# The first token block's attention, pair by pair of heads: a fused attention, dense and routed feed-forward kernel on one core

## The chip, the cores and the metric

One core of a Trainium2 chip runs the kernel. Its engines work side by side, each through its own instructions in order: TensorE (PE; PEld is its weight load), VectorE (DVE), ScalarE (ACT), GpSimd (POOL), and SyncE (SP), which here only issues DMAs. The metric is the device time of one execution in microseconds (us); the median of three timed executions of the kernel before is 759.19 us (756.44 to 760.04).

## The reference, cut to what matters

```python
def _attn_ref(q, k, v, g_norm):                     # q, k, v: 4 batches, 8 heads, 576 tokens, 64 wide
    kv = np.einsum('bhsd,bhse->bhde', k, v)
    out = np.einsum('bhsd,bhde->bhse', q, kv)
    rms = np.sqrt(np.mean(out * out, axis=-1, keepdims=True) + 1e-06)
    return (out / rms * g_norm).astype(np.float32)
...
def _moe_ref(x, w_in, w_out):                       # x: 2304 tokens x 512, w_in: 512 x 2048
    h = x @ w_in
    r = np.maximum(h, 0.0)
    return ((r * r) @ w_out).astype(np.float32)
...
    x = np.ascontiguousarray(attn_out.transpose(0, 2, 1, 3)).reshape(B * S, H * D)
    x = _moe_ref(x=x, **moe_kwargs)
    return _moe2_ref(x=x, **moe2_kwargs)            # eight experts, one per token, capacity 576
```

## The kernel before

The 2304 tokens are cut into six blocks of 384 (three tiles of 128). The first phase has, for each block, linear attention and then the dense feed-forward network with its 16 chunks `f` of the hidden layer; the second phase is the routed layer. Only the first block's start is touched by the change.

**Attention.** Two heads make a pair, so there are four pairs (`NPAIR`). `load_kv(0, p)` loads a pair's k and v (320 KB each), `load_q(t)` a tile's q for all pairs (256 KB). `kv(0, p)` makes a pair's 128 by 128 product in five matmuls and copies its two diagonal blocks to `kvb`, one by ScalarE (L212), one by VectorE (L213). Then, tile by tile and for all four pairs at once: `attn_out(t)` multiplies q with `kvb` (L228), ScalarE squares the result (L236), VectorE sums the squares per head (L238), GpSimd makes the mean and its power of -1/2 (L240, L242); `attn_mul(t)` scales (L246, VectorE); `attn_tr(t)` transposes on TensorE (L255) and leaves the block `xT` in two parts, a rounded one by ScalarE (L259) and the remainder by VectorE (L260).

**Weights.** The dense layer's weights come as 64-bit floats. `cvt_m(f)` turns the two tiles of chunk `f` (w_in and w_out, 128x512 each) to 32 bits: ScalarE scales the high words (L168, one each), VectorE has three kinds of integer operation (L169 and L170 on both tiles at once, 1024 columns; L174 for each). `split_m(f)` makes a rounded part (ScalarE, L183) and the remainder (GpSimd, L184). `mm1(s)` is a unit of the first product: twelve matmuls (L274), which need `xT` and both parts of w_in; its activation goes ScalarE, VectorE, ScalarE, VectorE (L282, L284, L285, L286); `mm2(s)` (L293) follows two units later. Units run (0, 0) to (0, 3), and from there chunks of blocks 0 and 1 alternate.

**What sets the order.** In this part only SyncE's queue stands as written; the other engines' orders are chosen by a scheduler when the program is built, and each engine then runs its own list in order. SyncE has at most eight loads under way.

Of the kernel before, what the change touches and what calls it, by code (L numbers as in the profile page):

```python
# [26 lines left out]
def attn_moe_kernel(ctx: ExitStack, tc: tile.TileContext, cap, kp, vp, qt, gn, wm, wg, wgt, w1, w2, ident, tri, out):  # L27
# [84 lines left out]
    def after_scatters(dma):  # L112
        dma = getattr(dma, "ins", dma)
        for i in scattered["disp"]:
            tc.add_manual_dep(
                dma, i.name, mybir.DependencyInfo(mybir.DependencyClass.Sync, mybir.DependencyReason.DATA),
                reason="reads what the scatters wrote",
            )

# [31 lines left out]
    def cvt_m(f):  # L151


        ws = [stg.pop(("m", f, i)).bitcast(I32).rearrange("p (n t) -> p n t", t=2) for i in range(2)]
        if f < 12:
            h = wpool2.tile([P, 2, 512], F32, tag="w", name="ch")
            o = wpool2.tile([P, 2, 512], F32, tag="w", name="cf")
            parts = [(h, o, slice(0, 2))]
            cvt[f] = [o[:, i, :] for i in range(2)]
        else:  # L160
            hs = [(apool1, apool)[i].tile([P, 1, 512], F32, tag="qx"[i], name="ch") for i in range(2)]
            os = [(apool, apool1)[i].tile([P, 1, 512], F32, tag="kv"[i], name="cf") for i in range(2)]
            parts = [(hs[i], os[i], slice(i, i + 1)) for i in range(2)]
            cvt[f] = [o[:, 0, :] for o in os]
        for h, o, sl in parts:
            hi, oi = h.bitcast(I32), o.bitcast(I32)
            for n, w in enumerate(ws[sl]):
                nc.scalar.activation(out=h[:, n, :], in_=w[:, :, 1].bitcast(F32), func=AF.Copy, scale=2.0 ** -112)  # L168
            nc.vector.tensor_scalar(oi, hi, -(1 << 31), None, op0=ALU.bitwise_and)  # L169
            nc.vector.scalar_tensor_tensor(  # L170
                out=oi, in0=hi, scalar=3, in1=oi, op0=ALU.logical_shift_left, op1=ALU.bitwise_or
            )
            for n, w in enumerate(ws[sl]):
                nc.vector.scalar_tensor_tensor(  # L174
                    out=oi[:, n, :], in0=w[:, :, 0], scalar=29, in1=oi[:, n, :],
                    op0=ALU.logical_shift_right, op1=ALU.bitwise_or,
                )

    def split_m(f, pool):
        os = cvt.pop(f)  # L180
        for o, d in zip(os, (wi, wo)):
            w = d[f] = pool.tile([P, 2, 512], F32R, tag="w", name="w")
            nc.scalar.copy(w[:, 0, :], o)  # L183
# [22 lines left out]
    def kv(b, p):  # L206
        k, v = kt.pop((b, p)), vt.pop((b, p))
        ps = misc()
        for c in range(NCH):
            nc.tensor.matmul(ps[:, :P], lhsT=k[:, c, :], rhs=v[:, c, :], start=c == 0, stop=c == NCH - 1)  # L210
# [54 lines left out]

    gt = {}

    def mm1(s):
# [3 lines left out]
        for c in range(KD):  # L272
            for a, m in PASSES:
                nc.tensor.matmul(  # L274
# [3 lines left out]
                n += 1  # L278

# [250 lines left out]
    with tc.manual_schedule(engines={mybir.EngineType.SP}):  # L530
# [16 lines left out]
        for p in range(NPAIR):  # L547
            load_kv(0, p)
            if p == 0:
                nc.sync.dma_start(out=id_sb, in_=ident)  # L550
                nc.sync.dma_start(out=gn_sb, in_=gn)
        for t in range(TB):
            load_q(t)
        load_m(0)
# [10 lines left out]
        for p in range(NPAIR):  # L565
            kv(0, p)
        for t in range(TB):
            attn_out(t)
        for t in range(TB):
            attn_mul(t)  # L570
            attn_tr(t)
        for f in range(2):
            cvt_m(f)
            split_m(f, wpool)
# [102 lines left out]
        for s in range(len(units)):  # L677
# [6 lines left out]
            if j == 0 and f + 2 < NF:  # L684
                cvt_m(f + 2)
# [8 lines left out]
            for p_ in plan.pop(s, []):  # L694
                p_()
            fl = s - at[NB - 1, 0]
# [379 lines left out]
```

## Time and profile before

| | |
|---|---|
| timed executions, median | 759.19 us (756.44 to 760.04) |
| profiled execution | 755.1 us |
| its span, first to last instruction | 753.2 us |
| mean granted TensorE clock in it | 0.991 of full |
| PE, DVE, ACT, POOL busy, share of the span | 95%, 49%, 41%, 39% |

The profiled execution is 1.9 us longer than its span and is the fastest of the four. The shares are means over stages with different limits: over the span TensorE is nearly always busy, but the first 72 us are another matter, and all of the change lies in these.

### The profile page before, as it was taken

The numbers are of one execution on the slowest core, as the hardware profiler recorded it, in microseconds if no ns is written. First come the engines' busy times: TensorE is split into PE (matmuls) and PEld (weight loads), VectorE is DVE, ScalarE is ACT, GpSimd is POOL, SyncE is SP. The second block draws the span as 40 slices with busy tenths as digits, with TensorE's granted clock in tenths as the row PEclk, the third lists the DMA queues.
The fourth block names the chain that finished last, engine by engine and source line by source line (L and its number), as shares of the span: only waits on it lengthen the run. The fifth ranks groups of instructions, "written<-read, shape, count | busy, mean of one in ns | idle before, by whom it ended". The sixth has DMA issues, their size and how long they took to land. (4 is left out here: it accounts for less than half of the span.)

```text
span 753.2 us, 12061 instructions
## 1 busy us (share of the span) xinstructions
PE 715.7 (95%) x4012; PEld 637.5 (85%) x4012; DVE 371.6 (49%) x833; ACT 309.5 (41%) x650; POOL 292.3 (39%) x288
## 2 busy tenths in 40 slices
PE   6678999999999999999999999999999999999985
PEld 6667999898899989989898988897888898889764
DVE  2989866548982594349634973331043221133011
ACT  2455454323222332233233264244276544376362
POOL 2566333112022200220130089043469746386881
PEclk9899999999999999999999999999999999999999
DMA  9946798401032202210010176043537554456530
GB/s 326 378 169 201 264 364 293 150 15 67 1 112 87 67 1 70 88 29 0 15 57 1 49 241 204 26 150 121 171 102 219 199 170 148 149 188 212 180 129 19
DMA packets 38016, 102.36 MB, mean 136 GB/s; under 512 B 4451, under 2 KB 4707, under 8 KB 37920
## 3 DMA queue, kind: packets, MB, share of 16 engines
q1 hardware_dynamic: 34912, 91.99, 36.4%
q0 software_dynamic: 3008, 9.10, 3.2%
q8 instruction: 59, 0.97, 0.5%
q14 instruction: 37, 0.30, 0.1%
HBM read 77.78 MB, written 23.91 MB: 135 GB/s over the span
## 5 line engine op out<-in xcount | busy, mean ns | idle before, releaser
L274 PE MATMUL pk<-xT,w 128*128 128x384 f32 x1152 | 223.1, 341 | 8.5 <-POOL w L184 4.6
L293 PE MATMUL pk<-w,g 128*128 128x512 f32 x864 | 218.4, 394 | 2.5 <-ACT g L285 2.5
L274 PEld LDWEIGHTS pk<-xT,w 128*128 128x128 f32 x1152 | 201.5, 188 | 18.6 <-POOL w L184 5.8
L195 POOL TENSOR_TENSOR w<-st,w 128x512 fp32r<-128x512 f32 x128 | 161.5, 1295 | 83.1 <-ACT w L191 83.0
L293 PEld LDWEIGHTS pk<-w,g 128*128 128x128 f32 x864 | 160.2, 188 | 31.7 <-ACT g L285 3.1
L282 ACT ACTIVATE rr<-pk 128x384 f32<-128x384 f32 x96 | 47.1, 492 | 153.6 <-PE pk L274 153.4
L817 PE MATMUL hb<-x,w 128*128 128x256 f32 (+2 forms) x672 | 96.7, 303 | 0.3
L817 PEld LDWEIGHTS hb<-x,w 128*128 128x128 f32 x672 | 93.8, 189 | 1.1 <-issue 0.2
L284 DVE TENSOR_TENSOR pk<-pk,rr 128x384 f32<-128x384 f32 x96 | 54.0, 563 | 74.6 <-ACT rr L282 73.7
L871 DVE SCALAR_TENSOR_TENSOR g<-hb,g 128x576 fp32r<-128x576 f32 (+3 forms) x72 | 40.5, 585 | 97.5 <-ACT g L870 96.5
L103 POOL DMA_INDIRECT disp<-y,sli x18 | 19.1, 1059 | 173.0 <-DVE sli L410 52.9
L355 DVE SCALAR_TENSOR_TENSOR junk<-y,wgb 128x512 f32<-128x512 f32 x120 | 78.0, 684 | 0.7 <-ACT y L313 0.6
L191 ACT CAST w<-st 128x512 fp32r<-128x512 f32 x128 | 71.7, 620 | 13.8 <-DMA st<-in_w 13.4
L285 ACT CAST g<-pk 128x384 fp32r<-128x384 f32 x96 | 46.0, 480 | 72.6 <-DVE pk L284 71.0
L286 DVE TENSOR_TENSOR g<-pk,g 128x384 fp32r<-128x384 f32 x96 | 53.3, 556 | 36.7 <-ACT g L285 36.0
L184 POOL TENSOR_TENSOR w<-cf,w 128x512 fp32r<-128x512 f32 x32 | 47.3, 1494 | 60.9 <-ACT w L183 56.3
L903 PE MATMUL hb<-w,g 128*128 128x512 f32 x264 | 65.7, 407 | 3.1 <-DVE g L871 2.5
L903 PEld LDWEIGHTS hb<-w,g 128*128 128x128 f32 x264 | 50.0, 193 | 15.7 <-DVE g L871 3.4
L870 ACT ACTIVATE g<-hb 128x576 fp32r (+3 forms) x72 | 34.9, 513 | 33.9 <-PE hb L817 29.2
L103 POOL DMA_INDIRECT out<-o,meta x22 | 21.3, 970 | 42.0 <-ACT o L911 17.8
L919 DVE SCALAR_TENSOR_TENSOR o<-bk,meta,o 64x512 f32<-64x512 f32 x3 | 2.3, 752 | 69.5 <-ACT o L918 51.0
L240 POOL TENSOR_SCALAR ms<-ss 128x8 f32<-128x8 f32 x18 | 4.6, 254 | 77.6 <-DVE ss L238 77.3
(138 smaller groups left out, 648.8 us busy)
## 6 DMA issues: line engine op xcount, KB each, us to landing
st<-in_w SPq DMA_DIRECT2D x64, 512.0 KB
st<-in_wm SPq DMA_DIRECT2D x32, 512.0 KB
disp<-zrow SPq DMA_DIRECT2D x9, 1028.0 KB
xr<-disp SPq DMA_DIRECT2D x32, 257.0 KB
k<-in_kp SPq DMA_DIRECT2D x16, 320.0 KB
v<-in_vp SPq DMA_DIRECT2D x16, 320.0 KB
q<-in_qt SPq DMA_DIRECT2D x18, 256.0 KB
out<-zrow SPq DMA_DIRECT2D x9, 512.0 KB
```

The lines of the kernel that those rows point to most:

```text
L184: nc.gpsimd.tensor_tensor(w[:, 1, :], o, f32(w[:, 0, :]), op=ALU.subtract)
L191: nc.scalar.copy(w[:, 0, :], s[:, i, :])
L195: e.tensor_tensor(w[:, 1, :], s[:, i, :], f32(w[:, 0, :]), op=ALU.subtract)
L274: nc.tensor.matmul(h, lhsT=wi[f][:, a, c * P:(c + 1) * P], rhs=xT[j][:, m, c, :], start=n == 0, stop=n == 3 * KD - 1,)
L282: nc.scalar.activation(out=r, in_=h, func=AF.Relu)
L284: nc.vector.tensor_tensor(h, h, r, op=ALU.mult)
L285: nc.scalar.copy(g[:, 0, :], h)
L286: nc.vector.tensor_tensor(g[:, 1, :], h, f32(g[:, 0, :]), op=ALU.subtract)
L293: nc.tensor.matmul(ysets[j == 1][i], lhsT=g[:, a, i * P:(i + 1) * P], rhs=wo[f][:, m, :], start=f == 0 and n == 0, stop=f == NF - 1 and n ...
L355: nc.vector.scalar_tensor_tensor(out=junk, in0=yt[j * TB + i][:, :DM], scalar=1.0, in1=wgb[e // 2][:, e % 2, :], op0=ALU.mult, op1=ALU.mul ...
L817: nc.tensor.matmul(h, lhsT=w1_at(e, f // 2, a, c)[:, f % 2 * P:(f % 2 + 1) * P], rhs=x[:, m, c, o:o + w], start=k == 0, stop=k == 3 * KD - 1,)
L903: nc.tensor.matmul(ps[:k, :], lhsT=lhs(f, a), rhs=we2[e, f][:, b, :], start=n == 0, stop=n == len(passes) * NF2 - 1,)
```

## The change

The first block's attention goes pair by pair instead of tile by tile. The three q tiles are loaded right after the first pair's k and v, ahead of the other three pairs. New functions treat one pair over all three tiles (384 tokens): `first_out` (product, square), `first_red` (sum of squares and power, on 6 columns instead of 8), `first_mul`, `first_tr` (three transposes and the rounded part of `xT`), `first_low` (the remainder). Their order is written out by hand, and the whole first section, up to the first chunk's weights, now stands as written on every engine. The first chunk's conversion is cut into its two tiles (512 columns each), w_in's put between pair 2's and pair 3's last steps. `in_order` keeps the later conversions behind the attention on ScalarE, and the second batch's `kv` products behind the first unit of `mm1` on TensorE.

```diff
+    def in_order(later, first):
...
+        tc.add_manual_dep(
+            later, first.name, mybir.DependencyInfo(mybir.DependencyClass.NoSync, mybir.DependencyReason.SCHED_ONLY),
...
-            parts = [(h, o, slice(0, 2))]
+            parts = [(h[:, a:a + n], o[:, a:a + n], slice(a, a + n)) for a, n in (((0, 1), (1, 1)) if f == 0 else ((0, 2),))]
...
+            if "kv" in marks:
+                in_order(a, marks["kv"])
...
+    def first_out(p):
+        ps = ops[p] = misc()
+        for t in range(TB):
+            nc.tensor.matmul(
+                ps[:, t * P:(t + 1) * P], lhsT=qtt[t][:, p, :], rhs=kvb[0][:, p, :],
+                start=t == 0, stop=t == TB - 1, skip_group_check=True,
+            )
...
+        nc.scalar.activation(out=x, in_=ps[:, :BT], func=AF.Square)
+
+    def first_red(p):
...
+        nc.vector.tensor_reduce(out=ss, in_=x.rearrange("p (h e) -> p h e", e=DH), axis=AX.X, op=ALU.add)
...
+        nc.gpsimd.tensor_scalar(ms, ss, 1.0 / DH, 1e-6, op0=ALU.mult, op1=ALU.add)
...
+        nc.gpsimd.tensor_tensor(r, ms, expo[:, :2 * TB], op=ALU.pow)
+
+    def first_mul(p):
...
+        nc.vector.tensor_tensor(
+            xst[p].rearrange("p (h e) -> p h e", e=DH), ps[:, :BT].rearrange("p (h e) -> p h e", e=DH),
...
+    def first_tr(p):
...
+        for t in range(TB):
+            nc.tensor.transpose(ps[:, t * P:(t + 1) * P], x[:, t * P:(t + 1) * P], id_sb)
...
+        marks["first"] = nc.scalar.activation(out=d[:, 0, p, :], in_=ps[:, :BT], func=AF.Copy, scale=gn_sb)
...
+    def first_low(p):
+        d, ps = xt_tile(0), ops.pop(p)
+        nc.vector.scalar_tensor_tensor(
+            out=d[:, 1, p, :], in0=ps[:, :BT], scalar=gn_sb, in1=f32(d[:, 0, p, :]), op0=ALU.mult, op1=ALU.subtract,
+        )
...
-    with tc.manual_schedule(engines={mybir.EngineType.SP}):
+    with tc.manual_schedule():
...
+        load_kv(0, 0)
+        nc.sync.dma_start(out=id_sb, in_=ident)
+        nc.sync.dma_start(out=gn_sb, in_=gn)
         for t in range(TB):
             load_q(t)
+        load_kv(0, 1)
+        load_kv(0, 2)
+        load_kv(0, 3)
...
+        free[:] = pk[2:8]
+        kv(0, 0)
+        first_out(0)
+        first_red(0)
+        first_mul(0)
+        first_tr(0)
+        kv(0, 1)
+        first_low(0)
+        first_out(1)
+        first_red(1)
+        kv(0, 2)
+        first_out(2)
+        first_mul(1)
+        first_red(2)
+        first_tr(1)
+        kv(0, 3)
+        first_low(1)
+        first_out(3)
+        first_mul(2)
+        first_red(3)
+        first_tr(2)
+        first_low(2)
+        c_in, c_out = cvt_m(0)
+        c_in()
+        split_m(0, wpool, (0,))
+        first_mul(3)
+        first_tr(3)
+        first_low(3)
+        c_out()
+        split_m(0, wpool, (1,))
...
+    with tc.manual_schedule(engines={mybir.EngineType.SP}):
+        marks["cvt"] = marks["first"]
+        for c in cvt_m(1):
+            c()
+        split_m(1, wpool)
+        marks["cvt"] = marks["split"]
```

What stands on TensorE from the first `kv` product to the first unit of `mm1`, before:

```order
L210 MATMUL pk_93<-v,k 128x128 x5
L210 MATMUL pk_94<-v,k 128x128 x5
L210 MATMUL pk_95<-v,k 128x128 x5
L210 MATMUL pk_93<-v,k 128x128 x5
L228 MATMUL pk_94<-kvb_128,q 128x128 x4
L228 MATMUL pk_95<-kvb_128,q 128x128 x4
L228 MATMUL pk_93<-kvb_128,q 128x128 x4
L255 MATMUL pk_94<-id_sb,x 128x128 x4
L255 MATMUL pk_95<-id_sb,x 128x128 x4
L255 MATMUL pk_93<-id_sb,x 128x128 x4
```

And of the change, on the same place (L224 is `kv`, L286 `first_out`, L314 `first_tr`, L334 `mm1`; pair 0 has the first three rows):

```order
L224 MATMUL pk_90<-v,k 128x128 x5
L286 MATMUL pk_91<-kvb_128,q 128x128 x3
L314 MATMUL pk_92<-id_sb,x 128x128 x3
L224 MATMUL pk_93<-v,k 128x128 x5
L286 MATMUL pk_94<-kvb_128,q 128x128 x3
L224 MATMUL pk_95<-v,k 128x128 x5
L286 MATMUL pk_90<-kvb_128,q 128x128 x3
L314 MATMUL pk_91<-id_sb,x 128x128 x3
L224 MATMUL pk_92<-v,k 128x128 x5
L286 MATMUL pk_93<-kvb_128,q 128x128 x3
L314 MATMUL pk_94<-id_sb,x 128x128 x3
L314 MATMUL pk_95<-id_sb,x 128x128 x3
```

Pair 1's `kv` product now stands behind pair 0's transposes and pair 3's behind pair 1's, where before all four stood ahead of every transpose; the four products of the second batch (L210, four times five) have moved from here to behind the first unit of `mm1`.

On VectorE, before, from the last `kvb` copy to the first chunk's last conversion step (`ch` and `cf` are the conversion's tiles):

```order
L213 COPY kvb_128<-pk_93 64x64
L238 TENSOR_REDUCE ss<-x 128x8 x2
L246 TENSOR_TENSOR x<-pk_94,r 128x512
L238 TENSOR_REDUCE ss<-x 128x8
L246 TENSOR_TENSOR x<-pk_95,r 128x512
L169 TENSOR_SCALAR cf<-ch 128x1024
L260 SCALAR_TENSOR_TENSOR xT<-pk_94,gn_sb,xT 128x4x128
L260 SCALAR_TENSOR_TENSOR xT<-pk_95,gn_sb,xT 128x4x128
L246 TENSOR_TENSOR x<-pk_93,r 128x512
L170 SCALAR_TENSOR_TENSOR cf<-ch,cf 128x1024
L169 TENSOR_SCALAR cf<-ch 128x1024
L260 SCALAR_TENSOR_TENSOR xT<-pk_93,gn_sb,xT 128x4x128
```

And of the change, from pair 1's scaling to pair 3's remainder (L229 `kvb` copy, L297 reduce, L305 scaling, L321 remainder, L183, L184 and L188 conversion):

```order
L305 TENSOR_TENSOR x<-pk_94,r 128x384
L297 TENSOR_REDUCE ss<-x 128x6
L229 COPY kvb_128<-pk_92 64x64
L321 SCALAR_TENSOR_TENSOR xT<-pk_91,gn_sb,xT 128x384
L305 TENSOR_TENSOR x<-pk_90,r 128x384
L297 TENSOR_REDUCE ss<-x 128x6
L321 SCALAR_TENSOR_TENSOR xT<-pk_94,gn_sb,xT 128x384
L183 TENSOR_SCALAR cf<-ch 128x512
L184 SCALAR_TENSOR_TENSOR cf<-ch,cf 128x512
L188 SCALAR_TENSOR_TENSOR cf<-st_176,cf 128x512
L305 TENSOR_TENSOR x<-pk_93,r 128x384
L321 SCALAR_TENSOR_TENSOR xT<-pk_95,gn_sb,xT 128x384
```

Each pair's sum of squares stands behind the scaling of the pair before it, and of the conversions only three operations on one tile (512 columns) stand ahead of the last remainder, where before three of 1024 columns did.

## Rows read from the trace of the kernel before

**Rows 1.** The page's head and its first part, busy us and share.
```profile
span 753.2 us, 12061 instructions
PE 715.7 (95%) x4012; PEld 637.5 (85%) x4012; DVE 371.6 (49%) x833; ACT 309.5 (41%) x650; POOL 292.3 (39%) x288
```
**Rows 2.** Stretches: length; PE, PEld, DVE, ACT, POOL busy (x); PEclk; DMA share; GB/s.
```profile
0.00:20.00 20.00, 13.15 (x86) 12.19 (x86) 5.75 (x17) 5.68 (x11) 4.89 (x13) 0.99 0.92 330
20.00:47.20 27.20, 21.18 (x130) 18.82 (x131) 24.07 (x33) 14.18 (x30) 13.99 (x13) 0.89 0.87 324
47.20:72.00 24.80, 19.62 (x95) 16.19 (x96) 23.18 (x29) 13.66 (x26) 18.05 (x12) 1.00 0.51 170
72.00:120.00 48.00, 48.00 (x244) 43.72 (x243) 35.34 (x52) 23.90 (x48) 16.37 (x12) 1.00 0.86 297
```
**Rows 3.** TensorE in order of time: start, us, instruction, xcount, idle before.
```profile
5.05 1.63 PE L210 MATMUL pk<-v,k 128*128 128x128 f32 x10
7.70 1.35 PE L210 MATMUL pk<-v,k 128*128 128x128 f32 x10 [1.02 <-DMA v<-in_vp]
11.44 1.35 PE L210 MATMUL pk<-v,k 128*128 128x128 f32 x10 [0.24 <-DMA v<-in_vp]
12.63 3.00 PE L228 MATMUL pk<-kvb,q 128*128 128x128 f32 x24
18.11 0.63 PE L255 MATMUL pk<-id_sb,x 128*128 128x128 f32 x4 [2.49 <-DVE x L246]
20.12 1.08 PE L255 MATMUL pk<-id_sb,x 128*128 128x128 f32 x4 [1.38 <-DVE x L246]
31.16 2.39 PE L274 MATMUL pk<-xT,w 128*128 128x384 f32 x12 [0.63 <-POOL w L184]
71.28 1.66 PE L293 MATMUL pk<-w,g 128*128 128x512 f32 x6 [2.47 <-ACT g L285]
```
**Rows 4.** ScalarE and GpSimd in order of time.
```profile
13.88 0.60 ACT L236 ACTIVATE x<-pk 128x512 f32<-128x512 f32 x1 [0.84 <-PE pk L228]
15.56 1.68 POOL L242 TENSOR_TENSOR r<-ms,expo 128x8 f32<-128x8 f32 x1
19.20 0.53 POOL L632 MEMSET zrow<- 128x514 f32 x1
24.58 0.69 ACT L259 ACTIVATE xT<-pk,gn_sb 128x512 fp32r<-128x512 f32 x1 [1.55 <-PE pk L255]
29.73 9.91 POOL L184 TENSOR_TENSOR w<-cf,w 128x512 fp32r<-128x512 f32 x6 [7.51 <-ACT w L183]
```
**Rows 5.** VectorE in order of time.
```profile
13.07 0.23 DVE L213 COPY kvb<-pk 64x64 f32<-64x64 f32 x1 [1.37 <-ACT kvb L212]
14.50 0.69 DVE L238 TENSOR_REDUCE ss<-x 128x8 f32<-128x512 f32 x1 [1.21 <-ACT x L236]
25.30 0.75 DVE L260 SCALAR_TENSOR_TENSOR xT<-pk,gn_sb,xT 128x512 fp32r<-128x512 f32 x1 [0.26 <-ACT xT L259]
27.17 1.22 DVE L170 SCALAR_TENSOR_TENSOR cf<-ch,cf 128x1024 int32<-128x1024 int32 x1
28.68 1.29 DVE L174 SCALAR_TENSOR_TENSOR cf<-st,cf 128x512 int32<-128x512 int32 x2
31.70 2.20 DVE L170 SCALAR_TENSOR_TENSOR cf<-ch,cf 128x1024 int32<-128x1024 int32 x1
33.94 3.34 DVE L174 SCALAR_TENSOR_TENSOR cf<-st,cf 128x512 int32<-128x512 int32 x2
46.62 0.55 DVE L286 TENSOR_TENSOR g<-pk,g 128x384 fp32r<-128x384 f32 x1
47.09 0.68 DVE L169 TENSOR_SCALAR cf<-ch 128x1024 int32<-128x1024 int32 x1
53.83 0.69 DVE L246 TENSOR_TENSOR x<-pk,r 128x512 f32<-128x512 f32 x1 [0.94 <-POOL r L242]
56.01 2.07 DVE L170 SCALAR_TENSOR_TENSOR cf<-ch,cf 128x1024 int32<-128x1024 int32 x1
```

More of the change, by code (lines that the diff above doesn't have):

```diff
@@ L118, in after_scatters @@
             )
+    def in_order(later, first):
+        later, first = getattr(later, "ins", later), getattr(first, "ins", first)
+        tc.add_manual_dep(
+            later, first.name, mybir.DependencyInfo(mybir.DependencyClass.NoSync, mybir.DependencyReason.SCHED_ONLY),
+            reason="the order in which the loads come in",
+        )
+    marks = {}
     kt, vt, qtt = {}, {}, {}
@@ L164, in cvt_m, with cvt_part, split_m @@
             cvt[f] = [o[:, 0, :] for o in os]
[L165 to L169, printed above, removed]
+        return [lambda part=part: cvt_part(ws, *part) for part in parts]
+    def cvt_part(ws, h, o, sl):
+        hi, oi = h.bitcast(I32), o.bitcast(I32)
+        for n, w in enumerate(ws[sl]):
+            a = nc.scalar.activation(out=h[:, n, :], in_=w[:, :, 1].bitcast(F32), func=AF.Copy, scale=2.0 ** -112)
+            if "cvt" in marks:
+                in_order(a, marks["cvt"])
+        nc.vector.tensor_scalar(oi, hi, -(1 << 31), None, op0=ALU.bitwise_and)
+        nc.vector.scalar_tensor_tensor(
+            out=oi, in0=hi, scalar=3, in1=oi, op0=ALU.logical_shift_left, op1=ALU.bitwise_or
+        )
+        for n, w in enumerate(ws[sl]):
             nc.vector.scalar_tensor_tensor(
-                out=oi, in0=hi, scalar=3, in1=oi, op0=ALU.logical_shift_left, op1=ALU.bitwise_or
-            )
[L173 to L183, printed above, removed]
+                out=oi[:, n, :], in0=w[:, :, 0], scalar=29, in1=oi[:, n, :],
+                op0=ALU.logical_shift_right, op1=ALU.bitwise_or,
+            )
+    def split_m(f, pool, which=(0, 1)):
+        for i in which:
+            o = cvt[f][i]
+            w = (wi, wo)[i][f] = pool.tile([P, 2, 512], F32R, tag="w", name="w")
+            marks["split"] = nc.scalar.copy(w[:, 0, :], o)
             nc.gpsimd.tensor_tensor(w[:, 1, :], o, f32(w[:, 0, :]), op=ALU.subtract)
@@ L209, in kv @@
         for c in range(NCH):
-            nc.tensor.matmul(ps[:, :P], lhsT=k[:, c, :], rhs=v[:, c, :], start=c == 0, stop=c == NCH - 1)
+            a = nc.tensor.matmul(ps[:, :P], lhsT=k[:, c, :], rhs=v[:, c, :], start=c == 0, stop=c == NCH - 1)
+            if "kv" in marks:
+                in_order(a, marks["kv"])
         d = kvb[b % 2]
@@ L273, in mm1 @@
             for a, m in PASSES:
-                nc.tensor.matmul(
+                a = nc.tensor.matmul(
                     h, lhsT=wi[f][:, a, c * P:(c + 1) * P], rhs=xT[j][:, m, c, :],
@@ L278, in mm1 @@
                 n += 1
+        if s == 0:
+            marks["kv"] = a
         r = gpool.tile([P, BT], F32, tag="rr", name="rr", bufs=2)
@@ L564, in attn_moe_kernel @@
             load_q(t)
-        for p in range(NPAIR):
-            kv(0, p)
-        for t in range(TB):
[L568 to L574, printed above, removed]
+        free[:] = pk[2:8]
[28 more added lines that the diff above has]
+        split_m(0, wpool, (1,))
+        for t in range(TB):
+            qtt.pop(t)
+        free[:] = ysets[1]
+    with tc.manual_schedule(engines={mybir.EngineType.SP}):
[4 more added lines that the diff above has]
+        marks["cvt"] = marks["split"]
         done_b = [1]
@@ L684, in attn_moe_kernel @@
             if j == 0 and f + 2 < NF:
-                cvt_m(f + 2)
+                for c in cvt_m(f + 2):
+                    c()
+                marks.pop("cvt", None)
                 split_m(f + 2, wpool if f + 2 < 12 else wpool2)
@@ L695, in attn_moe_kernel @@
                 p_()
+            if s == LEAD:
+                marks.pop("kv", None)
             fl = s - at[NB - 1, 0]
```

21 lines of the change are left out of this document (16 added, 5 removed).

## The prediction

> **What bounds the kernel now.** The page comes first: TensorE is busy for 95% of the span, the others for less than half of it [rows 1]. A mean says nothing about one stage, so the stretches are next [rows 2]. From 72 us on TensorE is busy throughout (48.00 of 48.00), and nothing that happens earlier on another engine can be made up there or lost there: a start that ends d us sooner should end the kernel d us sooner. Before 72 us it is otherwise. From 20 to 72 us VectorE is busy for 24.07 + 23.18 of 52.0 us, TensorE for 40.8, and TensorE's last long pause, 2.47 us before 71.28, ends with the activation `g` [rows 3], which waited its turn on VectorE. So from about 20 to 72 us the path runs through VectorE's list, and the question is when VectorE gets through it. A point to measure at is the end of the third unit's activation, at 46.62 + 0.55 = 47.17 us [rows 5]: by then four chunks of weights are converted, three units activated, the second batch's `kvb` copied. In the changed order the very same set is done when VectorE ends that same instruction, and from there on its list is nearly the same. I work out when that is.
>
> **The new attention, walked through.** Durations for 512 columns are cut to three quarters for 384, an estimate. The steps are: a pair's `kv` 1.35 on TensorE; the two copies, 0.5 from its end (11.44 + 1.35 to 13.07 + 0.23); the product with q 0.85 (24 passes took 3.00 in a row; here six, and the pipeline's end); square 0.45 to 0.5 (0.60); reduce 0.53 (0.69); 0.37 from there to the power's start; the power; the scaling 0.55; three transposes with their start 0.6; rounded part 0.55 (0.69); remainder 0.57 (0.75) [rows 3 to 5].
> The power on 6 columns stands nowhere. On 8 it takes 1.68 [rows 4]. From below it is bounded by 6/8 of that, 1.26 (nothing makes it dearer by the column when there are fewer), from above by 1.68. I take 1.3, near the lower end, since two-operand work of 512 columns takes GpSimd 9.91/6 = 1.65 us [rows 4], so that the eight powers' cost is mostly the power itself, paid by the column.
>
> Loads: a pair takes (11.44 - 7.70)/2 = 1.9 us, 640 KB. The q tiles, 768 KB, now follow pair 0, which is there at 5.05; at that pace they land at 7.3, at that of the first interval (2.65 for a pair and two small loads) at 8.2. I take 8.1. Pair 1 is then there at about 10.0, pair 3 at 13.7.
> - Pair 0: its last product ends at 8.5, square 9.0, reduce 9.6, power 11.3, scaling 11.9, transposes 12.5. Its `kv` was done at 6.7: it waits for q.
> - Pair 1: TensorE runs in order, and its `kv` is behind pair 0's transposes. It starts at 12.3, 2.3 us after its data. Copies 14.2, product 15.0, square 15.5, reduce 16.1, power 17.8, scaling 18.4, transposes 19.0.
> - Pair 2: its reduce is behind pair 1's scaling on VectorE: 19.0. On GpSimd three small operations now stand ahead of its power: the fill of `zrow` (0.53 [rows 4]), a copy into a row buffer that pair 1's transposes must first let go, and an index fill; about 0.65 us past the reduce. Power 21.25. VectorE meanwhile does pair 3's `kvb` copy and pair 1's remainder until 21.3; scaling 21.8, transposes 22.5.
> - Pair 3: `kv` behind pair 1's transposes, 18.85 to 20.2, with data since 13.7. Copies 20.7, product 21.6, square 22.1, reduce behind pair 2's scaling 22.7, power 24.4. VectorE, however, first does pair 2's remainder and w_in's three operations, halves of L169 (0.68) and L170 (1.22) and one L174 (0.65) [rows 5], from 23.8 to 25.4; scaling 26.0, transposes 26.6, rounded part 27.25, remainder 27.85.
>
> So the attention's last step ends at 27.9 where it ended at 25.30 + 0.75 = 26.05 [rows 5]: two pairs do wait behind others. The first unit of `mm1` still comes sooner. w_in's rounded part is ready at 26.1 and its remainder at 27.5 (the cast, then 1.3 on GpSimd), so the unit ends at about 29.8, against some 33.2 before (31.16 + ten of twelve in 2.39 [rows 3]): 3.4 us sooner. That alone does not shorten the kernel, since VectorE's list is what the following units wait for.
>
> **VectorE from there to the common point.** Before, from 26.05 to 47.17 it did 15.8 us of work at the prices of rows without a neighbour (two L174 of chunk 0, L170 and L174 of chunk 1, chunks 2 and 3 whole at 3.2 each, three activations, four copies, one reduce, one scaling), lost 3.0 where GpSimd's six subtractions ran at the same time (L170 2.20 for 1.22, the two L174 3.34 for 1.29 [rows 5]; the six are 9.91 in a row from 29.73 [rows 4]), and 2.3 to waits and a like slowing of L169. After 27.9 more of chunks 0 and 1 is left: half of L169 and L170 of w_out, chunk 1's L169, less one L174: 16.8. The subtractions no longer come as one row of six but in three pairs, of which by my walk about half lies beside conversions: 1.5 (bounds 0 and 3.0). Waits I leave at 2.3: ScalarE's conversions of chunk 1 now come behind the last rounded part, and those of chunk 2 behind four casts, which costs VectorE 0.35 and about 1.0, while the old waits on `g` shrink. 27.9 + 16.8 + 1.5 + 2.3 = 48.5, 1.3 later than 47.17.
> Behind the common point GpSimd is then about 2 us further on than it was, because its subtractions began sooner: the wait of 0.94 on its power at 53.83 [rows 5] should go. That leaves +0.4.
>
> **TensorE's clock.** Before, TensorE paused from 15.6 to 18.1 and had only transposes behind it; then the granted clock was at its lower level, 1.2 GHz, from which 0.89 as the mean of 20 to 47.2 us comes [rows 2], and four transposes took 1.08 instead of 0.63 [rows 3]. In the new order the pause comes earlier: 8.5 to 12.0, waiting for pair 0, again followed by transposes. If pair 1's `kv` and product then run at the lower level, 1.35 + 0.85 becomes some 3.9 by that ratio, +1.7 on the path. If the clock holds, nothing. I take 1.0, a little over the middle, the pause being longer than the one that cost it before. Of the Trainium skill, "TensorE: Matmul & The Clock Gate" (section "Why this matters for your kernels") advises against pauses between bursts of matmuls, since they bring back the lower clock; the trace agrees at 20 us. By that rule alone, without my halving, the sum would be 0.7 higher.
>
> **Edits costed at nothing.** Moving the second batch's `kv` behind the first `mm1` unit: TensorE waits there for chunk 1's remainder (31.16 had 0.63 of such a wait [rows 3]), and four times 1.35 fits into the 4 us until my walk has it; without that cover 5.4 us of TensorE's time would stand ahead of the second unit. Later weight loads: their buffers come free some 3 to 5 us later, as chunk 1 is converted later, but ScalarE reaches chunk 4 only at 46. The split of chunk 0 adds two starts of instructions on VectorE, about 0.1.
>
> **Sum.** Against the profiled execution: 755.1 + 0.4 + 1.0 = 756.5. That execution is 4 us under the timed median, 759.2; on the median's footing I say 760.6. The forecast's own bounds: -2.2 (contention gone, 1.5; clock holds, 1.0; q at 7.3, 0.8; power at 1.26, 0.1; 0.2 for rounding) to +4.7 (contention as before, 1.5; clock down throughout pair 1, 0.7; power at 1.68, three times 0.38 on the path, 1.1): 757.0 to 763.9.
>
> **Rivals.**
> 1. *VectorE and GpSimd get out of each other's way.* If the subtractions, spread out, fall beside no conversion, 1.5 more goes, and of four L170 between 47 and 72 us (2.07 in the row at 56.01 [rows 5]) 0.85 each could go as well, 3.4: +1.4 - 1.5 - 3.4 = -3.5, 755.7. For it: the six in a row are gone. Against it: conversion, cast and subtraction of successive tiles still follow each other, so the next conversion lies beside the last subtraction. It decides against my forecast if the L170s stay at 1.2. Chance 0.15. The Trainium skill's "GPSIMD Engine Reference" (section 1, Specifications) says that GpSimd shares its SBUF interfaces with VectorE and contends with instructions that have two SBUF inputs, as L170 and L174 have; 2.20 against 1.22 agrees.
> 2. *The pairs flow at the pace of their loads,* as the change's words have it. With pair 3's `kv` at 13.8 and its power unhindered its remainder would be done at about 21.5, w_in's conversion ahead of it included at 22.5: 5.4 sooner than in the walk, so -4.0 in all, 755.2. Against it is the order on TensorE itself; it needs pair 0's transposes done before pair 1 lands, at 10 us, so a chain from q to transposes of under 2 us where I have 4.4. Chance 0.05.
> 3. *Slower: the clock stays down for all of the attention.* Pair 3's `kv` and product, on the path through pair 1's remainder, then cost another 1.7, and pair 1's the full 1.7: +0.4 + 3.4 = +3.8, 763.0, and over that with any of the forecast's upper bounds. It decides from the point where pair 3's `kv` too runs at 1.2 GHz. For it: `kv`, product and transposes come in short bursts with pauses of a microsecond or more throughout. Against: between 6 and 13 us before there were such pauses too (1.02 at 7.70), and the clock held. Chance 0.20.
>
> The forecast itself has 0.60.
>
> **How the numbers follow.** Under about 0.5%, 3.8 us, a measurement of this kernel cannot tell a difference from none; the three runs alone differ by 3.6. Faster by more: rival 2 and half of rival 1, 0.13. Slower by more: half of rival 3, rounded up for what adds to it, and the forecast's upper edge, 0.13 + 0.05 = 0.18. Same: 0.69. The range takes in rivals 1 and 2 down to 755.0 and rival 3 up to 764.5, which leaves out what lies beyond their prices, under 2 in 10.
>
> **What the changed profile would show.** Right: pair 1's `kv` idle until pair 0's scaling, near 12; four powers 3 us apart from the second on; the last remainder after 26; the first `mm1` unit done by 31; the third unit's activation ending between 46 and 50; TensorE's last pause before 72 to 74. Wrong: a power on 6 columns far under 1.26; `kv` of pair 1 at 10; the clock at full throughout; L170 at 1.2 up to 72 us, with the common point well before 46.

## The result and the profile after

The changed kernel takes 762.96 us (median of 10 runs, 760.35 to 765.77); the kernel before, run beside it, 756.37 us (10 runs, 754.86 to 760.04). The ratio is 1.0076, 95% interval [1.0053, 1.0099]: **slower by 0.8%, 6.6 us**. The forecast was +1.4 us, no change that can be measured; rival 3 (the clock stays down for all of the attention, +3.8) is what happened, and more was lost beside it.

The profiled execution took 765.77 us, the slowest of the ten, while that of the kernel before, 755.1, lies near the low end of its ten; so the two traces differ by 10.7 us, not by 6.6. Its page has the same shape as [rows 1]:

```profile
span 764.0 us, 12068 instructions
PE 723.8 (95%) x4012; PEld 645.1 (84%) x4012; DVE 371.0 (49%) x838; ACT 310.2 (41%) x652; POOL 290.8 (38%) x290
```

The loss is in the first stretch. The windows of [rows 2] (start:end, length, busy time and instructions of each engine, granted clock) read now:

```profile
0.00:20.00 20.00, 13.20 (x62) 12.20 (x63) 4.05 (x13) 3.25 (x6) 2.36 (x11) 0.81 0.88 323
20.00:47.20 27.20, 20.50 (x111) 17.94 (x110) 19.06 (x33) 13.59 (x30) 11.55 (x13) 0.76 0.81 285
47.20:72.00 24.80, 22.09 (x123) 18.96 (x124) 23.80 (x31) 14.08 (x27) 18.64 (x14) 1.00 0.46 152
72.00:120.00 48.00, 45.52 (x222) 40.83 (x221) 36.14 (x50) 23.72 (x48) 18.03 (x13) 0.96 0.88 294
```

The granted clock is 0.81 and 0.76 where it was 0.99 and 0.89: by these shares 0.19 x 20 + 0.24 x 27.2 us are missing of full speed, so twice that, some 21 of the first 47 us, ran at 1.2 GHz. VectorE has 19.06 us of work done from 20 to 47.2 us where it had 24.07, and the fourth window now has a pause of TensorE in it. TensorE's timeline of the new attention, which answers to [rows 3] (start, duration, instructions, in brackets the idle time ahead and what ended it):

```profile
9.17 0.49 PE L286 MATMUL pk<-kvb,q 128*128 128x128 f32 x2 [0.16 <-DMA q<-in_qt]
13.21 0.88 PE L314 MATMUL pk<-id_sb,x 128*128 128x128 f32 x3 [3.54 <-issue]
13.87 2.34 PE L224 MATMUL pk<-v,k 128*128 128x128 f32 x10
16.77 1.65 PE L286 MATMUL pk<-kvb,q 128*128 128x128 f32 x6 [0.56 <-DVE kvb L229]
...
23.20 2.34 PE L224 MATMUL pk<-v,k 128*128 128x128 f32 x10
26.09 0.94 PE L286 MATMUL pk<-kvb,q 128*128 128x128 f32 x6 [0.55 <-DVE kvb L229]
...
31.45 0.87 PE L314 MATMUL pk<-id_sb,x 128*128 128x128 f32 x3 [3.70 <-DVE x L305]
31.97 4.46 PE L334 MATMUL pk<-xT,w 128*128 128x384 f32 x12
...
77.27 2.93 PE L355 MATMUL pk<-w,g 128*128 128x512 f32 x6 [2.48 <-ACT g L347]
```

Pair 0's product waits for its q tiles until 9.17 us. Its transposes come after a pause of 3.54 us, and behind it the `kv` of pairs 1 and 3 (pair 2's too) take 2.34 us instead of 1.35. Only at 26 us, with the product of pair 3 (0.94 after 1.65), is full speed back, and the next pause, 3.70 us ahead of pair 3's transposes, loses it again: the first `mm1` unit takes 4.46 us. GpSimd and VectorE, for [rows 4, 5]:

```profile
19.91 1.33 POOL L301 TENSOR_TENSOR r<-ms,expo 128x6 f32<-128x6 f32 x1
23.55 0.18 POOL L378 COPY y<-tok 128x1 int32<-128x1 int32 x1 [1.83 <-PE pk L314]
```

```profile
32.98 0.62 DVE L321 SCALAR_TENSOR_TENSOR xT<-pk,gn_sb,xT 128x384 fp32r<-128x384 f32 x1 [1.67 <-ACT xT L316]
47.90 2.20 DVE L184 SCALAR_TENSOR_TENSOR cf<-ch,cf 128x1024 int32<-128x1024 int32 x1
53.42 0.69 DVE L262 TENSOR_TENSOR x<-pk,r 128x512 f32<-128x512 f32 x1 [0.93 <-POOL r L258]
54.03 0.55 DVE L348 TENSOR_TENSOR g<-pk,g 128x384 fp32r<-128x384 f32 x1
```

The attention's last remainder ends at 33.59 us (27.9 forecast, 26.05 before), the third unit's activation at 54.58 (48.5 forecast, 47.17 before): VectorE needs 21.0 us from the one to the other, as it did before (21.1). What came late into its list came late out of it.

### The profile page after: what moved, and what is told of

It is laid out like the page before. It is cut to its first block, busy times and chain, and to the rows that moved or that the text cites. A ratio compares the mean times of both kernels' runs of the same rounds, so it can differ in the third digit from the quotient of the medians.

```text
span 764.0 us, 12068 instructions
## 1 busy us (share of the span) xinstructions
PE 723.8 (95%) x4012; PEld 645.1 (84%) x4012; DVE 371.0 (49%) x838; ACT 310.2 (41%) x652; POOL 290.8 (38%) x290
## 4 chain that ended last, share of the span: by engine, by line
PE 70%; DMA 14%; POOL 4%; issue 4%; DVE 4%; ACT 2%; SPq 1%; POOLq 0%; ACTq 0%; DVEq 0%
PE pk L334 23%; PE pk L355 23%; DMA out<-o,meta 10%; PE hb L914 10%; PE hb L1000 6%; PE bk L1000 4%; DMA v<-in_vp 3%; POOL w L209 2%; PE pk L244 1%; PE pk L224 1%; POOL r L258 1%; DVE g L968 1%; DMA st<-in_wm 1%; PE bk L893 1%; PE pk L271 1%
## 5 line engine op out<-in xcount | busy, mean ns | idle before, releaser
L334 PE MATMUL pk<-xT,w 128*128 128x384 f32 x1152 | 225.8, 343 | 6.2 <-POOL w L198 3.1
L334 PEld LDWEIGHTS pk<-xT,w 128*128 128x128 f32 x1152 | 203.6, 190 | 16.6 <-POOL w L198 4.5
L209 POOL TENSOR_TENSOR w<-st,w 128x512 fp32r<-128x512 f32 x128 | 161.5, 1295 | 84.9 <-ACT w L205 47.2
L348 DVE TENSOR_TENSOR g<-pk,g 128x384 fp32r<-128x384 f32 x96 | 53.3, 556 | 35.9 <-ACT g L347 35.8
L198 POOL TENSOR_TENSOR w<-cf,w 128x512 fp32r<-128x512 f32 x32 | 44.6, 1407 | 62.5 <-ACT w L197 53.9
L1000 PE MATMUL hb<-w,g 128*128 128x512 f32 x264 | 64.1, 399 | 3.0 <-DVE g L968 2.4
```

Source lines behind the costliest of these rows:

```text
L209: e.tensor_tensor(w[:, 1, :], s[:, i, :], f32(w[:, 0, :]), op=ALU.subtract)
L334: a = nc.tensor.matmul(h, lhsT=wi[f][:, a, c * P:(c + 1) * P], rhs=xT[j][:, m, c, :], start=n == 0, stop=n == 3 * KD - 1,)
L348: nc.vector.tensor_tensor(g[:, 1, :], h, f32(g[:, 0, :]), op=ALU.subtract)
L1000: nc.tensor.matmul(ps[:k, :], lhsT=lhs(f, a), rhs=we2[e, f][:, b, :], start=n == 0, stop=n == len(passes) * NF2 - 1,)
```

## The experiments

Three marks tell each kernel's first stretch: the end of the last remainder, the end of the third unit's activation, and that of the sixth and seventh, which come in a row at TensorE's long pause past 70 us. Before they stand at 26.05, 47.17 and 72.70 us, after at 33.59, 54.58 and 78.69. VectorE's row of the third mark, in the trace of before:

```profile
71.69 1.01 DVE L286 TENSOR_TENSOR g<-pk,g 128x384 fp32r<-128x384 f32 x2
```

All times are medians with the interval of the ratio to the kernel before in the same job, whose median was 756.84, 755.78 and 756.35 us in the three jobs. Kernels of different jobs are compared by their ratios first, since the median of the kernel before moves by 1 us between them.

**Filling the pauses.** The first kernel keeps the change and has idle-time matmuls on zeros, result unused, ahead of three of the four groups of transposes:

```diff
+        def fill_pe(n):
+            for i in range(n):
+                nc.tensor.matmul(pk[0][:, :P], lhsT=cold, rhs=cold, start=True, stop=True)
...
+        fill_pe(13)
         first_tr(0)
...
+        fill_pe(5)
         first_tr(1)
...
+        fill_pe(13)
         first_tr(3)
```

> The changed kernel with 31 idle-time matmuls on a constant tile put on TensorE (13 ahead of pair 0's transposes, 5 ahead of pair 1's, 13 ahead of pair 3's), results unused. Clock theory (TensorE's pauses bring the clock to 1.2 GHz, and the products between the pairs then take twice as long): the granted clock stays at 1.0 to 36 us, the last remainder of the attention ends at 28.5 to 29.5 us instead of 33.6, the kernel gains 4 to 5 us on the changed one, ratio to before 1.001 to 1.004. Order theory (pairs wait behind each other's transposes and scalings, whatever the clock): the last remainder stays past 32 us and the ratio at 1.006 or more.

Measured: 759.85 us, 1.0046 [1.0025, 1.0067]. The windows of the first 47.2 us, TensorE and VectorE:

```profile
0.00:20.00 20.00, 16.63 (x117) 15.90 (x118) 5.29 (x16) 4.53 (x9) 4.96 (x15) 1.00 0.90 331
20.00:47.20 27.20, 22.36 (x153) 19.25 (x151) 22.94 (x35) 14.51 (x31) 12.62 (x12) 1.00 0.89 322
```

```profile
7.60 0.94 PE L286 MATMUL pk<-kvb,q 128*128 128x128 f32 x6 [0.56 <-DVE kvb L229]
8.37 3.07 PE L631 MATMUL pk<-cold 128*128 128x128 f32 x26
12.08 0.52 PE L314 MATMUL pk<-id_sb,x 128*128 128x128 f32 x3 [0.64 <-issue]
12.44 1.28 PE L224 MATMUL pk<-v,k 128*128 128x128 f32 x10
...
27.74 2.04 PE L334 MATMUL pk<-xT,w 128*128 128x384 f32 x10 [0.56 <-POOL w L198]
```

```profile
27.47 0.62 DVE L321 SCALAR_TENSOR_TENSOR xT<-pk,gn_sb,xT 128x384 fp32r<-128x384 f32 x1 [1.32 <-ACT xT L316]
...
48.50 0.55 DVE L348 TENSOR_TENSOR g<-pk,g 128x384 fp32r<-128x384 f32 x1
...
72.11 1.01 DVE L348 TENSOR_TENSOR g<-pk,g 128x384 fp32r<-128x384 f32 x2
```

The clock is 1.00 in both windows, pair 1's `kv` takes 1.28, and the marks stand at 28.09, 49.05 and 73.12 us: 5.5 us sooner than in the changed kernel. Not all of this is the clock's: in this execution the q tiles have landed when pair 0's product starts at 7.60, and its transposes start at 12.08 instead of 13.21. From there to the last remainder the changed kernel takes 20.4 us and this one 16.0; the 4.4 us between them are the clock's. By the medians, the kernel with matmuls added to TensorE's program is 3.1 us faster, by the ratios 2.3; these two intervals overlap, and the gain stays below the 4 to 5 us expected. The lower clock is not the profiled execution's alone: the mean granted clock is 0.977 to 0.984 in the ten executions of the changed kernel, 0.984 to 0.993 in the twelve of this one, and 0.982 to 0.993 in the 71 of the kernel before in the three jobs.

**The same count without the filling.** Since the filled kernel has 31 instructions more on TensorE, this one has 31 too, but small ones behind the warm-up, and leaves the pauses as they are:

```diff
         for i in range(HOT):
             nc.tensor.matmul(pk[0][:, :P], lhsT=cold, rhs=cold, start=True, stop=True)
+        for i in range(31):
+            nc.tensor.matmul(pk[0][0:16, :16], lhsT=cold[:, :16], rhs=cold[:, :16], start=True, stop=True)
```

> The changed kernel with 31 small matmuls behind the warm-up, so with the count of the filled kernel but with the pauses left as they are. Clock theory: the clock falls from 12 us as in the changed kernel, the third unit's activation ends at 53.5 to 55.5, and the time is 762 to 765, 3 us or more over the filled kernel's 759.85. Rival (the filled kernel gained by its instruction count, not by the clock): 759 to 761.

Measured: 764.09 us, 1.0092 [1.0062, 1.0123]. The two windows have clocks of 0.85 and 0.86, the last remainder ends at 31.70 and the third activation at 52.70:

```profile
8.93 0.94 PE L286 MATMUL pk<-kvb,q 128*128 128x128 f32 x6 [0.56 <-DVE kvb L229]
13.41 0.52 PE L314 MATMUL pk<-id_sb,x 128*128 128x128 f32 x3 [3.55 <-issue]
```

```profile
20.00:47.20 27.20, 20.03 (x120) 17.54 (x120) 21.03 (x34) 13.83 (x30) 13.16 (x14) 0.86 0.88 307
```

```profile
31.08 0.62 DVE L321 SCALAR_TENSOR_TENSOR xT<-pk,gn_sb,xT 128x384 fp32r<-128x384 f32 x1 [1.67 <-ACT xT L316]
52.15 0.55 DVE L348 TENSOR_TENSOR g<-pk,g 128x384 fp32r<-128x384 f32 x1
```

It is 0.8 us under the expected stretch; the time is as expected. At equal count the filling is worth 0.46% by the two ratios, 3.5 us, or 4.2 by the two medians; with the two intervals taken as independent, an estimate of 0.7 to 6.3. So the gain comes from the filling, not from the count, and its size is loosely known. At the first two marks it is 3.6 us. Of these, 1.3 stand ahead of the transposes, which start at 13.41 here: the small matmuls push pair 0's product from 7.60 to 8.93. The other 2.3 us are the clock's, which fell for less time here than in the changed kernel's trace.

**Filling with no instruction more.** Wider matmuls (384 columns), three for the warm-up instead of nine, and two, one and three ahead of the transposes of pairs 0, 1 and 3:

```diff
-    HOT = 9
+    HOT = 3
...
-            nc.tensor.matmul(pk[0][:, :P], lhsT=cold, rhs=cold, start=True, stop=True)
+            nc.tensor.matmul(pk[0][:, :BT], lhsT=cold[:, :P], rhs=cold, start=True, stop=True)
...
+        fill_pe(2)
         first_tr(0)
```

> The changed kernel with matmuls of 384 columns: three as warm-up in place of nine of 128, and two, one and three ahead of the transposes of pairs 0, 1 and 3, so that TensorE's program has exactly as many instructions as before and after. Clock theory: the clock holds for most of the attention, the last remainder ends at 28 to 29.5 us instead of 33.6, the third unit's activation at 49 to 50.5, and behind it all is as in the changed kernel: 757.5 to 759.5. Rival (the clock is not what the changed kernel loses): 762 to 764.

Measured: 760.06 us, 1.0059 [1.0038, 1.0080]; clocks 0.91 and 0.94, marks at 30.40, 51.38 and 75.50 us. The pauses are filled in part, the clock comes back in part, and the marks lie between those of the changed and of the filled kernel. The first two marks and the time are 0.6 to 0.9 us beyond the upper edges expected.

**Another order of the pairs.** Here pair 1's `kv` no longer stands behind pair 0's transposes, nor pair 3's behind pair 1's, and pair 2's reduce stands ahead of pair 1's scaling:

```diff
         first_red(0)
+        kv(0, 1)
         first_mul(0)
         first_tr(0)
-        kv(0, 1)
-        first_low(0)
         first_out(1)
+        first_low(0)
...
         first_out(2)
+        first_red(2)
+        kv(0, 3)
         first_mul(1)
-        first_red(2)
         first_tr(1)
-        kv(0, 3)
-        first_low(1)
         first_out(3)
+        first_low(1)
```

> The changed kernel with pair 1's kv product put ahead of pair 0's transposes, pair 3's ahead of pair 1's, and pair 2's reduce ahead of pair 1's scaling; nothing added. Order theory: kv and copies of pairs 1 and 3 (2.9 us each at the lower clock) leave the path, the last remainder ends near 28 us, ratio to before 1.000 to 1.003. Clock theory: the clock is still down from about 12 us, kv is hidden but products, transposes and the first unit of the dense layer stay at double price, the last remainder ends near 31 us, ratio 1.004 to 1.006.

Measured: 760.50 us, 1.0058 [1.0038, 1.0078]. In the profiled execution, an unusually slow one (765.89 us), the clock was 0.75 up to 20 us and the first two marks stood at 32.69 and 53.69: 0.9 us sooner than after. The order alone does not free the pairs while TensorE runs at 1.2 GHz; the median's gain of 2.5 us, 1.4 by the ratios, is within the intervals. The clock fell here although no pause of TensorE from its first products up to 20 us was longer than 1.19 us: pair 1's `kv`, after a pause of 1.18, already took 2.50 us at 10.50. The same order with 8, 3, 4 and 8 idle-time matmuls ahead of the four groups of transposes:

> Both edits (the order of e2, 23 idle-time matmuls). If both theories hold in part: clock at 1.0 throughout, last remainder near 26 us as before the change, ratio 0.997 to 1.001. If only one of them matters it is no better than the better of the other two.

Measured: 764.23 us, 1.0112 [1.0080, 1.0143], the slowest of all, although its marks are 27.34, 48.70 and 74.30 us. From pair 0's transposes (12.92) to the last remainder it takes 14.4 us, 1.6 less than the filled kernel: so much does the new order lose at full clock by pairs that wait behind each other. The kernel before, filled alike (10, 5 and 9 ahead of its three tiles' transposes, with TensorE's order there fixed by hand):

> The kernel before with 24 idle-time matmuls between its tiles' transposes (10, 5, 9), order otherwise as it was. The clock stays at 1.0 from 19 to 26 us. Clock theory: half a us to 1.5 us to gain, ratio 0.998 to 0.9995, since only transposes and part of one kv product stood in that stretch. Order theory: no change, 1.000.

Measured: 762.29 us, 1.0074 [1.0046, 1.0103] (the ratio leaves out one execution of 3998 us), with marks at 28.08, 47.99 and 73.49 us. The edit changed more than the clock: the scheduler has put other operations ahead on VectorE. The last scaling ends at 22.57, 0.7 us sooner than before, but two L174 of chunk 0 (from 25.97 before) now stand ahead of the last remainder, so the first mark isn't like for like:

```profile
25.54 1.28 DVE L174 SCALAR_TENSOR_TENSOR cf<-st,cf 128x512 int32<-128x512 int32 x2
27.34 0.74 DVE L272 SCALAR_TENSOR_TENSOR xT<-pk,gn_sb,xT 128x512 fp32r<-128x512 f32 x1
```

Against marks that lie at most 1.6 us behind those of before at the seventh activation, both kernels lose most of their time, 4 to 6 us, far behind the attention. In the second of them TensorE pauses for 2.57 us at 523 us, in the first for 1.95, and in the kernel before it does not:

```profile
517.34 1.08 PE L796 MATMUL bk<-id_sb,xr 128*128 128x128 f32 x8 [1.34 <-issue]
518.70 5.86 PE L903 MATMUL hb<-w,g 128*128 128x512 f32 x24 [0.28 <-ACT x L801]
```

```profile
520.52 1.08 PE L902 MATMUL bk<-id_sb,xr 128*128 128x128 f32 x8 [1.33 <-issue]
523.55 7.42 PE L1009 MATMUL hb<-w,g 128*128 128x512 f32 x24 [1.95 <-ACT w L205]
```

The first fence is the kernel before, the second the other order filled; 24 matmuls behind the pause take 7.42 us instead of 5.86, since the clock falls there. The releasers that the trace names differ from kernel to kernel, though the old order filled has the same instructions in the same order there as the kernel before. Behind this pause the other order filled falls from 3.2 to 6.3 us behind the kernel before, the old order filled from 2.1 to 5.7.

**Only the count.** The kernel before with 24 small matmuls behind the warm-up, and nothing else (the added lines are those above, with 24):

> The kernel before, with 24 small matmuls (16 columns, result unused) behind the nine warm-up matmuls, in time in which TensorE waits for its first loads anyway; all else as before. Two kernels with 23 and 24 added matmuls showed a new pause of TensorE of 2.0 to 2.6 us near 523 us, and a stretch at 1.2 GHz behind it, though nothing of the program differs there; one with 31 had neither. Theory 1 (the pause depends on how many instructions stand ahead in TensorE's program, not on what the first 50 us do): the pause is here too, near 519 us, and the time is 759.5 to 761 against 756.8. Theory 2 (the pause comes from what happens around the attention): no such pause, 756 to 758.

Measured: 760.97 us, 1.0063 [1.0038, 1.0088]. Its marks are even 0.8 us sooner than before (46.36 for the third activation), and yet it loses 5 us. TensorE, and the page's line of the queue that loads instructions (packets, MB, share), whose first number is 59 in the kernel before:

```profile
518.24 1.08 PE L798 MATMUL bk<-id_sb,xr 128*128 128x128 f32 x8 [1.48 <-issue]
522.17 5.05 PE L905 MATMUL hb<-w,g 128*128 128x512 f32 x14 [2.84 <-DVEq L929]
```

```profile
q8 instruction: 60, 0.98, 0.5%
```

Of all thirteen traces (with before and after) the three with 23 or 24 added instructions have 60 such packets and this pause; the ten with none or 31 have 59 and no such pause. Two more kernels test it from the other side. The other order, filled, with eight small ones more, so 31:

> The changed kernel in the other order with 23 idle-time matmuls (764.2 us), and eight more small ones behind the warm-up, so that 31 are added, as in the filled kernel that had no pause near 520 us. Theory 1 (the pause hangs on the count of instructions ahead of it): pause and slow stretch go, 759.5 to 761. Theory 2 (it comes from the order of the pairs): pause stays, 763 to 765. In both the attention's last remainder ends at 27 to 28 us and the third unit's activation at 48.5 to 49.

Measured: 760.40 us, 1.0043 [1.0022, 1.0065], so 3.8 us less by the medians, 5.2 by the ratios, for eight instructions more. The marks, 29.37, 50.35 and 75.88, are later than expected, since pair 0's transposes start at 14.95 instead of 12.92; the 14.4 us from there are the same. There is no pause:

```profile
522.12 1.08 PE L904 MATMUL bk<-id_sb,xr 128*128 128x128 f32 x8 [1.48 <-issue]
523.46 3.75 PE L1011 MATMUL hb<-w,g 128*128 128x512 f32 x15 [0.27 <-ACT x L909]
```

And the kernel before with 31:

> The kernel before, with 31 small matmuls behind the warm-up: the same number of TensorE instructions as the kernels with 31 idle-time or leading matmuls. If that number costs nothing by itself, 755 to 757 as the kernel before, no pause near 520 us, and what those kernels lose against before is theirs. If the number costs something as 24 did (5 us), 758 to 761, and the filled kernel's loss of 3 us is mostly the number's.

Measured: 756.78 us, 1.0001 [0.9982, 1.0020]: 31 instructions cost nothing, 24 cost 5 us. Before and after have the same number of matmuls in their traces, 4012, and 59 packets both, so this effect is no part of the result; it is the reason why each filled kernel has to be compared at its own count.

**The held-back products.** The filled kernel without the rule that puts the second batch's `kv` behind the first `mm1` unit:

```diff
-        if s == 0:
-            marks["kv"] = a
```

> The changed kernel with idle-time matmuls (759.85 us), without the rule that holds the second batch's kv products back behind the first mm1 unit: 13 of their 20 matmuls now stand ahead of that unit, three of these ahead of pair 3's transposes. Prediction's step (costed at nothing, 5.4 us of TensorE without cover): the first mm1 unit ends 2 to 4 us later, but VectorE's list decides, so the third unit's activation ends within 1 us of the 49.05 of that kernel, and the time is 759 to 761. Rival (TensorE is what the first units wait for): the activation ends 3 to 5 us later, 763 to 765.

Measured: 759.61 us, 1.0056 [1.0037, 1.0076], as the filled kernel (759.85). The marks, however, are 32.13, 55.18 and 77.01: the third activation ends 6.1 us later than in the filled kernel. Some 1.9 of it are there at pair 2's remainder (25.72 for 23.86), before the rule matters, since the q tiles landed later and the first filling took 4.70 us instead of 3.07:

```profile
9.43 4.70 PE L629 MATMUL pk<-cold 128*128 128x128 f32 x26
```

The other 4.2 are what the rival said (3 to 5), but VectorE has more ahead of that activation here, among it two scalings of the second block instead of one, and a wait of 3.12 us on GpSimd. By the seventh activation 3.9 us are left, and the pause that stands at 71.70 us in the filled kernel, 2.47 us with a stretch at 1.2 GHz behind it, is 0.60 us here, with none. The time follows neither expectation alone: the marks moved as the rival said, the median did not:

```profile
70.18 1.21 PE L353 MATMUL pk<-w,g 128*128 128x512 f32 x4 [0.60 <-ACT g L345]
71.23 2.28 PE L334 MATMUL pk<-xT,w 128*128 128x384 f32 x12
```

**A cold start for the old order.** The kernel before with `HOT = 1` and eight small matmuls in place of the others:

> The kernel before with one warm-up matmul instead of nine (and eight of 16 columns, so that the count of instructions stays): TensorE begins its first products at 1.2 GHz. Theory 1 (it is the new order that makes the attention's chain hang on the clock: each pair's kv stands behind the transposes of the pair before): in the old order four kv of 2.35 end 1 to 3 us later, the last remainder by as much, and the third unit's activation ends at 47 to 49 us; 757 to 759. Theory 2 (a low clock in the first 25 us costs any order alike): the activation ends 4 us later or more, 761 to 763.

Measured: 755.81 us, 0.9994 [0.9979, 1.0008], under both expected ranges; marks 27.23, 47.83 and 73.34. Only pair 0 ran at half pace (first row); the other three, at the pace of their loads, follow in the second; the marks are 1.2 us later at first and 0.6 then:

```profile
4.73 2.47 PE L210 MATMUL pk<-v,k 128*128 128x128 f32 x10 [2.34 <-DMA v<-in_vp]
8.07 5.92 PE L210 MATMUL pk<-v,k 128*128 128x128 f32 x30 [0.87 <-DMA v<-in_vp]
```

So this says that the old order is not touched by a slow first pair, and little of what slow pairs behind it would do. A slow stretch the old order has of its own: 0.89 from 20 to 47.2 us [rows 2], and a lower one in this run, 0.82, in which the marks are no more than 1.2 us later and the median isn't longer.

## Why the prediction came out as it did

- **The path runs through VectorE's list** held. In the changed kernel, the filled one and those between, the third activation follows the last remainder by 21.0 to 21.4 us, against 20.6 forecast (16.8 + 1.5 + 2.3), wherever the remainder stands; the kernel whose second batch's products come early differs, and the filled old order, with another order on VectorE.
- **The walk** held at full clock. The filled kernel, in which the clock is 1.00, ends its last remainder at 28.09 (27.9 forecast) and its first `mm1` unit at 29.78 (29.8). The power on 6 columns takes 1.33 us (1.3 taken), pair 1's `kv` waits for pair 0's scaling, and the row copy on GpSimd waits for pair 1's transposes. The last q tile, put at 8.1, landed at 7.95 in the filled kernel and at 9.13 in the changed one.
- **The +0.4 left without the clock** held: the filled kernel's seventh activation ends at 73.12, 0.42 us behind the one before. The way there was not quite the forecast's: the third is 1.9 behind (1.3 forecast), the wait of 0.94 on the power did not go (0.93 at 53.42), and the rest is won between the third and the seventh.
- **The step that failed is the clock's term:** "I take 1.0, a little over the middle", with 0 to 1.7. From pair 0's transposes to the last remainder it measured 4.4 us in the changed kernel's trace and 2.3 in that with the same count, each against the filled kernel; in the medians at equal count 3.5 to 4.2, loosely. The price of one pair was right: `kv` and product took 2.34 + 1.65 instead of 1.28 + 0.94, 1.8 more (the 3.9 of the prediction should read 3.8 by its own ratio, 1.08 to 0.63). What it was applied to was not. The walk let the lower clock take pair 1's `kv` and product. It took the transposes of pairs 0 and 1, the `kv` of pairs 1 to 3 and the products of pairs 1 and 2, each of which stands ahead of the next on TensorE, and after the second pause pair 3's transposes and the first `mm1` unit. The reason given against, that the clock had held through a pause of 1.02 at 7.70 us, was no measure for a pause of 3.54; the pause of 2.49 us ahead of 18.11 us, after which the clock did fall, was the nearer row. The rule of the Trainium skill cited there ("TensorE: Matmul & The Clock Gate", section "Why this matters for your kernels"), followed without halving, was nearer the truth: the trace agrees with it, by 0.81 and 0.76 with pauses of 3.54 and 3.70 us. It too was applied to one pair only.
- **What happens behind 72 us** was the second thing wrong: "a start that ends d us sooner should end the kernel d us sooner". The changed kernel's trace is 6.0 us behind at the seventh activation and 10.8 at the end, the filled one's 0.42 and 5.3; where this goes is told below.
- **The number owes something to luck.** The forecast's 760.6 and its range up to 764.5 stand on 759.2, a median of three executions; ten gave 756.37. From there +1.4 is 757.8, rival 3's +3.8 is 760.2, and the range would end at 761.7, short of 762.96. It reached so far only because rival 3, at 0.20, was taken in; "slower by more" had 0.18. Of its signs, the first unit by 31 us, the third activation by 50 and the last pause by 74 failed in the changed kernel (36.43, 54.58, 77.27) and came out or nearly so in the filled one (29.78, 49.05, 71.70).
- **Rival 3** is confirmed, by its own sign: pair 3's `kv` at 2.34. Its 3.4 us for the clock lie between the 2.3 and 4.4 of the traces, though it left out pair 2's `kv`, the transposes and the `mm1` unit and counted pair 3's product, which ran at full speed; what is missing from its +3.8 lies behind 72 us. **Rival 1** is refuted: L170 (now L184) still takes 2.20 at 47.90 us. **Rival 2** is refuted: pair 3's `kv` ran at 23.20, with data since 14, and even in the other order at full clock the last remainder ended at 27.34, not 21.5.
- **Later weight loads** cost nothing that shows: up to 90 us no conversion on ScalarE waits for a load, in the changed kernel or the filled one. **The held-back products** cost nothing in the time, but not for the reason given; without the rule the first three units come later, and a pause with its slow stretch goes.

**Where the rest goes.** The filled kernel still loses 3 to 5 us in the medians where its trace shows 0.42 up to 73 us. The traces place it, by VectorE's last step of each unit (L286, now L348) and later of each unit of the routed layer, against the kernel before. The changed kernel is 6.0 us behind from the seventh activation to the tenth, 7.5 from the thirteenth (97 us before) to the end of the dense layer (477), 8.7 at 684 us before and 10.8 at the end; the filled one 0.4, 1.8, 2.8 and 5.3. The first step is a stretch at 1.2 GHz behind the pause of 2.47 us at 71 to 78 us, which makes the next six matmuls take 2.93 instead of 1.66 [rows 3]; the filled kernel's row comes first here. The second lies at another such stretch, near 490 us, shown in the kernel before, the changed one, and the kernel before with 31 small matmuls:

```profile
71.70 2.93 PE L355 MATMUL pk<-w,g 128*128 128x512 f32 x6 [2.47 <-ACT g L347]
```

```profile
485.23 1.64 PE L772 MATMUL hb<-w 128*128 128x512 f32 x6
492.74 2.12 PE L869 MATMUL hb<-w 128*128 128x512 f32 x6
486.95 2.33 PE L774 MATMUL hb<-w 128*128 128x512 f32 x6
```

The third, behind 720 us, has TensorE waiting for ScalarE as well as a slow stretch. The last of these kernels, with the old order, loses the same in its profiled execution (760.12 us, the slowest of its twelve): 0.2, 1.7, 2.9 and 5.1 us behind. But its median of 756.78 says that most of its executions don't.

**What stays open.** The walk's 0.4, 2.3 to 4.4 for the clock in the attention and 1.5 at the pause near 72 us add up to 4.2 to 6.3 of the 6.6; this sum is of traces, and no one run shows it. All seven traces of the changed order that have that pause have the stretch behind it, and of five of the old order two. Why the old order is spared more often isn't settled: of each kernel one execution is profiled, and a kernel that fills that pause alone wasn't tried, since it changes the order of what follows.

## What to carry to other kernels

Where a walk of dependent steps puts short bursts of matmuls behind pauses (of 3.5 us here, and in the other order of 1.2), price every burst on the chain at 1.2 GHz and every one at 2.4, and take the first unless a row shows the clock holding through such a stretch. Breaking a stage into pieces that each wait for one another trades a few long pauses for many short bursts, and the clock makes most of the price; matmuls on zeros in the pauses won back about 3 us here. Compare traces from the first step that the change concerns, since the landing of one load moved the marks by 1 us. And when an experiment adds instructions, run the same number of idle ones beside it, since the count alone moved this kernel by 5 us.

## What was not expected of the hardware

- Twenty-four small matmuls at the start of TensorE's program make the kernel before 5 us slower, though its first marks come no later; thirty-one make no difference. The trace of the slow ones has one packet more in the queue that loads instructions (60 for 59) and a pause of 2.0 to 2.8 us some 515 us later, with a stretch at 1.2 GHz behind it. That the extra load causes the pause is the reading that fits all thirteen traces, not one that was tried apart.
- In the cold start the ten matmuls of pair 0 took 2.47 us, twice their later 1.28, while the granted clock of 0 to 20 us reads 0.99: the half pace at the start of this run does not show in that column.
